# Keys of two early projections in shared PSUM banks, the second input loaded in two halves, and a new order of the first steps

## The chip, the cores and the metric

The kernel runs on one core of a Trainium2 chip. A core has five engines that work side by side, each through its own list of instructions in order: TensorE (PE, matrix products into PSUM), VectorE (DVE), ScalarE (ACT, exponentials and copies), GpSimd (POOL, here products in SBUF) and SyncE (SP, which here only issues transfers). Transfers between HBM and SBUF run on 16 DMA engines. An engine waits on semaphores for results of the others. The metric is the time of one execution on the device in microseconds (us); lower is better.

## The reference

Attention with random features, and then a soft mixture of experts over its result:

```python
def phi(x):
    proj = np.einsum('bhsd,df->bhsf', x, w_phi)
    proj = proj - np.max(np.abs(proj), axis=-1, keepdims=True)
    return np.concatenate([np.exp(proj), np.exp(-proj)], axis=-1)
q_p, k_p = (phi(q), phi(k))
kv = np.einsum('bhsf,bhsd->bhfd', k_p, v)
z = np.sum(k_p, axis=2)
num = np.einsum('bhsf,bhfd->bhsd', q_p, kv)
den = np.einsum('bhsf,bhf->bhs', q_p, z)[..., None] + 1e-06
x = num / den                                # as (4608, 512)
...
logits = x @ phi                             # 32 slots
slot_input = softmax_over_tokens(logits).T @ x
h = np.maximum(slot_input[e] @ w1[e], 0.0)   # 8 experts, 4 slots each
slot_out[e] = h @ w2[e]
out = softmax_over_slots(logits) @ slot_out
```

q, k and v have 8 batches, 8 heads, 576 tokens and 64 columns; there are 128 random features. The change touches the start of the attention only.

## The kernel before, in words

The host packs k and q, transposed, into 37 inputs `xT[e]` of 128 partitions by 1024 columns (512 KB; the first is loaded in its two used quarters, 128 KB each). Input e feeds the projections 2e (columns 0 to 511) and 2e + 1 (columns 512 to 1023). A projection (`proj`, matmuls on L281) makes the keys of four token tiles, and the queries of the four tiles that lie two projections back: `proj` b writes keys `kx[b]` into a PSUM bank of the pool `psk`, which has two, and from b = 2 on queries `qx[b - 2]` into a bank of `mm` (two as well). The halves of the 128 partitions hold keys and queries and trade places with each projection.

What follows for the keys of one projection b:

- `kneg_exp` b (ACT, L312), `kmax` b (DVE, L286, the largest absolute value per token) and `kpos_exp` b (ACT, L315) read the bank. No two engines read one bank at a time: for the first two projections the order is `kneg_exp`, `kmax`, `kpos_exp`. The two exponentials make the tile `kf`.
- `kfac` b (ACT, L289 and L290) takes exponentials of the maxima, into `mk`.
- `vals` p (POOL, L301) multiplies value tiles `vt[u]` (325 KB of input for one head of two batches, loaded by `vload` u) with `mk`, into `vs`. The pieces 0, 1 and 2 are the four, four and one tiles of the first head; pieces 3 and 4 begin the second.
- `kvmm` p (PE, L328) multiplies `kf` with `vs` and sums into `kvp`; `kvcopy` takes the sum out after piece 2.

Queries go through `qpos` (ACT, L348), `qabs` (DVE, L343) and `qneg` (ACT, L351), again one after the other on their bank, then `num` (PE, L381) multiplies them with the copied sum, and DVE and POOL finish the attention. Later PE turns the tokens, makes logits, runs both expert layers (L850, L925) and the output (L945).

Three more PSUM banks are shared (`bank3`, tokens `nm`: one in the pool `pmo`, two in `pnum`): whoever takes one gets the one that came free longest ago. The results of `num`, the transposes and logits use them. `spin` (L206) is a matmul on a constant (`warm`) whose result nobody reads: nine stand at the very start, in banks of `mm`, and eight more (`NSPIN`) among the first steps, in the shared banks.

The order is written out by hand. Each letter of the string `ORDER` issues the next task of one kind; `LETTERS` says which. Every engine runs its tasks in the order of the string. The planner `Plan` hands out tokens for buffers and banks and checks that the listed predecessors were issued; the costs and due times in the calls of `add` are not used when the order is given. On the chip the waits follow from what the tiles share. Before, the first steps are on PE: `proj` 0, 1, six spins, `proj` 2, a spin, `proj` 3, `kvmm` 0, 1, a spin, `kvmm` 2, `proj` 4, 5; on ACT: `kneg_exp` 0, 1, `kpos_exp` 0, `kfac` 0, 1, `kpos_exp` 1, `qpos` 0, `kneg_exp` 2, `qpos` 1, `qneg` 0, `kfac` 2, `kpos_exp` 2, `kneg_exp` 3, `qneg` 1, `kpos_exp` 3, `kneg_exp` 4; on DVE: `kmax` 0, 1, `qabs` 0, `kmax` 2, 3, `qabs` 1.

The first transfers are issued before the string is run: on SP's queue the quarters of input 0 (L197, L199) and the whole input 1 (`xload(1)`, L174); on ACT's queue the projection matrix `wd` (L198) and value tile 0 (L189). Inputs 2 and 3, value tile 1 and so on follow on SP's queue.

Of the kernel before, what the change touches and what calls it, by code (L numbers as in the profile page):

```python
# [9 lines left out]
F32 = mybir.dt.float32  # L10
# [6 lines left out]
B, H, S, D = 8, 8, 576, 64  # L17
# [5 lines left out]
NCH = NT // CH  # L23
# [5 lines left out]
XW = 8 * 128  # L29
# [9 lines left out]

NB = NU * NT // 4  # L40
NWARM = 9
NSPIN = 8
NFIN = 3
TRI = 3
BUFS = {'xs': 3, 'kf': 3, 'vs': 2, 'vt': 2, 'qf': 3, 'un': 2, 'xT': 4, 'xc': 2}
# [11 lines left out]
class Plan:  # L57
# [10 lines left out]
    def add(self, kind, key, engine, cost, fn, after=(), get=(), put=(), lat=0.0, at=0, mode=None):  # L68
        get, put = ([(g, None) if isinstance(g, str) else g for g in x] for x in (get, put))
        self.tasks.setdefault(kind, []).append((key, fn, after, get, put))  # L70
# [29 lines left out]
ORDER = (  # L100
    "bcceafeefedhdggehjibecikbajelfcmdbmdknghjefomilcbunhfipoghclrjqddlrmkjagmjsnbkifnthijgvovmwcljofpwqdgcrvrmkjwnlm"
    "yhksomfdpnathixrvwvczolijwgfcrlhaqkdAvAgrmjnAbkwfbyomstizhcArfvwnlkjnAdorimdavAgcowhjpiqvcgwdfbmhgjyrlrdslxjztvf"
    "AknmivhiknawgowmcofjplcAhrjrAmdvqwxdlgjiykfrnakmgmostcvnbhpvjiwwlfocdjzqsArlvhkntrgbmdwAAvwomkfigcdryjharvznfkmi"
    "bowcvlpwjrghAqrmdnlijAAykofsmnhiczotxjvwgkdlvcfmgAwjqfjparrhsdmnmvgAtwAojlxihmkvyzwnorvjwpbrvwcfAixckmybdfazAnrh"
    "AdgliABABgjljCoqxcBCskhtBCmilmnfCdrDEkonvchpFwgvlwqoibcrrjdjkafbAnmhodsvkmwBitgCBcBvwCxlBylCfrnhfjrivmvhCwjDGdzx"
    "oEcwaqkipsndoFcgglHGjHIJrIymfKhKkAgldnqgbtLisojmArAvwfhkvimtpnjcojwzcrfalhvdgrmdwlkfAAnmAbjmJvwhoprkvMwyirjgjzcv"
    "wnlyAoifcdamdkqAnmlhixgzfoxsAtjrhjLviwrcgvlbmknoArfawvAjpqwxhycmklfbmnshrkdzidAtnorvcwAlivggjocmfajwrqMAprjdvhwk"
    "mknsdiynmgrAtzjfAogclvAwhoAljfiqdvgcwmrhkjpdvsftwxlnryvmgimazwrhkbjvowrnaiAvAmjpwocckymfnzdbAAhrdglBNjlCBgoiqCkf"
    "cBbsBAjmthAifmlnCrCdkhnvjiwxvwoDcoaEcBpbFbdgflBjxhrdCrNmvqxmskfnwCiBlCBhtgCojicaGxvfklDrnwdohxOrEkgnjFqvwiymvpcw"
    "gocHjHdzmIfgyrzJGkIsdlKLhnKmAfArjhlAmtvwiovAkiwAcnAjobacpqdgfglsrrvhmfjbknltwvOwmdyrvkjjgnraxvwimwzphocikocdfyrl"  # L110
    "ghirAdjqnlkszPxAAmfonojtmjvhwigmcvwdMjpcNArrflagkdmqhnsimfgljAkhAmvtwjopcfvyrJwjbirlanqdzkmAmAvvhnocsoAMiwtwbgcf"
    "yzbAjralNlfvhwAkrdiAmdkpnbxnvoghroqvjgwjcwdfsligycxtrdkzhvrminmvoAfjlmawgjcrfLApwlbjhvkqwryhmkAminzonAsBBcodticA"
    "gCCvdfjwBCfBrlrhlCAdkvniokhmjvnqxiwbDgwcoOEcFBBprlglsajytdmCmvjmxqknCfwPzHpgBIBjChmCrsjdgjfoPJvrkiDwhvEwKncFiMbd"
    "fGAohcHLylrtlgkaIqmAmJndsgKoijcfAzvwrdNkpvfwnrbvmAwahjhlirogAAtriknvjwvcwGyfOljzxkdonoxcmmghlqpriAvwbkrbjdysxAmA"
    "tznrcfhvgkndvwiwjofcaAlAlmmrhgpqdAkvfrjmwsnMohriitayLckvocvnwgrkdwnvjwxmjzffAglmplocyhjhAzNocxxAAqRldSRlmjrsmgkS"
    "APjOtPvmqprwvRrwSnvwiOTURsAQRkSotyrSnRvoVQwRVzrSSrvwyyTAARUzPASvzARXASwyXRYzA4XZYSY0X2QYZ0TZ73W905Q5682236573Q5+"
    "695W5888++8/W+<=/Q!=!i!!")

# [7 lines left out]
def tile_kernel(ctx: ExitStack, tc, xT, vv, w, phi, w1, w2, cst, out):  # L126
# [46 lines left out]
    def load(t, x):  # L173
        i = nc.sync.dma_start(t, x).ins  # L174
        if len(sent) > 5 and len(wpools) < 2:
            tc.add_manual_dep(i, sent[-2].name, mybir.DependencyInfo(mybir.DependencyClass.Sync, mybir.DependencyReason.DATA), reason="deep")
        sent.append(i)
# [3 lines left out]
    def xload(e):  # L181
        if e > 2:
            xs[e] = xtile(e)
        if e:
            load(xs[e], xT[e])

    def vload(u):
        vt[u] = vp.tile([128, VW], F32, tag="vt", name="vt", bufs=BUFS["vt"])
        load(vt[u], vv[u // H, u % H]) if u else nc.scalar.dma_start(vt[u], vv[u // H, u % H])  # L189


    call = const.tile([128, NTT, NS], F32, name="call")
# [3 lines left out]
    wd = qp.tile([128, FE], F32, name="wd", bufs=1)  # L196
    nc.sync.dma_start(xs[0][0:64, 0:512], xT[0][0:64, 0:512])  # L197
    nc.scalar.dma_start(wd, w)  # L198
    nc.sync.dma_start(xs[0][64:128, 512:XW], xT[0][64:128, 512:XW])  # L199
    vload(0)  # L200
    xload(1)
    nc.gpsimd.memset(call[:, 0:2], 0.0)
    warm = call[:, 0:2].rearrange("p t s -> p (t s)").bitcast(mybir.dt.bfloat16)

# [61 lines left out]
    def proj(b):  # L266
        half = slice(0, 64), slice(64, 128)
        kh, qh = half[::-1] if b % 2 else half
        if b < NB:
            kx[b] = pkp.tile([128, 4, 128], F32, tag="psk", name="psk")  # L270
        if b > 1:
            qx[b - 2] = pmm.tile([128, 4, 128], F32, tag="mm", name="psq")
        x = xs[b // 2].rearrange("p (t i) -> p t i", i=128)[:, 4 * (b % 2):4 * (b % 2) + 4]
        for i in range(4):
            two = []
            if b < NB:
                two.append((kx[b][:, i], x[kh, i], wd[kh]))
            if b > 1:
                two.append((qx[b - 2][:, i], wd[qh], x[qh, i]))
            for ps, l, r in two[::-1] if b % 2 else two:  # L280
                nc.tensor.matmul(ps, l, r, start=True, stop=True)  # L281
# [351 lines left out]
    def zsi(i):  # L633
        nc.vector.tensor_copy(si[:, 2 * i:2 * i + 2], fin["st", i][:, 0:2])
        if i:
# [3 lines left out]


    plan = Plan(dict({k: BUFS[k] for k in ("kf", "vs", "qf", "un", "xT", "xc", "vt")}, xs=BUFS["xs"] - 2, psk=2, psq=2,
                     kb0=1, kb1=1, qb0=1, qb1=1, pkv=1, kvs=2, psn=2, mo=2, mk=6, mh=1, eq=3, dn=3, lT=3, de=2,
                     cd=3, pl=2, pr=3, nm=3))
    add = plan.add

    for e in range(NB // 2 + 1):
        first = e < 2
        add("load", e, SP, 1.35 if e else 1.43, (lambda: None) if first else lambda e=e: xload(e), lat=2.2, at=8 / 3 * e,
            get=[] if first else ["xs"], after=[("vload", 0)] if e == 1 else [])
    for u in range(NU):  # L650
        add("vload", u, SP, 0.85, lambda u=u: vload(u) if u else None, after=[] if u == 0 else [("load", 1)], lat=2.2, at=NCH * u, get=["vt"])

    for b in range(NB + 2):
        def task(kind, engine, cost, fn, key, bank, **k):
            add(kind, key, engine, cost, lambda: fn(key), at=4 / 3 * bank, **k)
        task("proj", PE, 0.896 if 1 < b < NB else 0.77, proj, b, b, after=[("load", b // 2)], lat=0.34, mode="r", get=["psk"] * (b < NB) + ["psq"] * (b > 1), put=["xs"] * (b % 2))
        bank = [f"kb{b % 2}"]
        if b < NB:
            task("kmax", DVE, 0.6, kmax, b, b, after=[("proj", b)], get=["mk"] + bank, put=bank, lat=0.16)
            task("kfac", ACT, 0.19, kfac, b, b, after=[("kmax", b)], lat=0.21)  # L660
            task("kneg_exp", ACT, 0.478, kneg_exp, b, b, after=[("proj", b)], get=["kf"] + bank, put=bank, lat=0.13)
            task("kpos_exp", ACT, 0.478, kpos_exp, b, b, after=[("kneg_exp", b)], get=bank, put=bank)
            task("kread", None, 0.0, lambda b: None, b, b, after=[("kmax", b), ("kpos_exp", b)], put=["psk"], lat=0.0)
        for p, (b_, u, t0, t1) in enumerate(pieces):
            if b_ == b:
                new, end = t0 == 0 or p == 0 or pieces[p - 1][0] != b, 4 * b + 4 == NT * u + t1
                n = t1 - t0
                mid = t0 <= 4 < t1
                task("vals", POOL, 0.14 * (1 + (mid and t1 > t0 + (t0 == 4))) + 0.22 * (n + mid), vals, p, b,
                     after=[("kfac", b), ("vload", u)] + ([] if pieces[p - 1][0] != b else [("vals", p - 1)]),  # L670
                     get=["vs"] * (p == 0 or pieces[p - 1][0] != b), put=["mk"] * end + ["vt"] * (t1 == NT))
                task("kvmm", PE, 0.233 * n + 0.215 * mid, kvmm, p, b, after=[("kpos_exp", b), ("vals", p)] + ([("kvmm", p - 1)] if p else []),
                     get=["pkv"] * (t0 == 0), put=["kf", "vs"] * end, mode="c", lat=0.25)
        q, bank = b - 2, [f"qb{b % 2}"]
        if q >= 0:
            task("qabs", DVE, 0.63, qabs, q, q, after=[("proj", b)], get=bank, put=bank, lat=0.16)
            task("qpos", ACT, 0.478, qpos, q, q, after=[("proj", b)], get=bank + ["qf"], put=bank, lat=0.13)
            task("qneg", ACT, 0.478, qneg, q, q, after=[("qpos", q)], get=bank, put=bank, lat=0.13)
            task("qread", None, 0.0, lambda b: None, q, q, after=[("qabs", q), ("qneg", q)], put=["psq"], lat=0.0)
# [111 lines left out]
        task("wdiv", POOL, 0.36, wdiv, n, after=[("wsum", n)], put=["cd"])  # L791

    for i in range(NSPIN):
        add("spin", i, PE, 0.22 if i > 1 else 0.43, lambda: spin(bank3("spin", [128, 512], "psw"), warm), after=[("proj", 0)], get=["psn", ("nm", "spin")], put=["psn", ("nm", "spin")], lat=0.0, at=1e6)
    add("consts", 0, SP, 0.75, constants, after=[("proj", 4)], at=15, lat=2.5)
    for i in range(nslot[0]):
        add("weight", i, SP, 1.3, lambda: load_w(1), after=[("consts", 0)], at=1000)
# [216 lines left out]
```

## Time and profile before

| | us |
|---|---|
| median of 3 timed runs | 329.48 |
| lowest and highest of them | 328.75, 329.61 |
| profiled execution, its own time | 328.39 |
| its span, first to last instruction | 326.6 |

All times inside the kernel are from the span's start in that one execution. The page of the profile has the busy time and the idle time of groups of instructions; the trace behind it gives the chain of waits (followed back from the last instruction), the timeline, the transfers with their time from issue to landing, and busy times in chosen stretches. In rows of stretches the numbers stand for start and end, length, busy time with the count of instructions of PE, PE's weight loads, DVE, ACT and POOL, then the granted PE clock, the DMA engines' busy share and GB/s. In a row of the timeline the first number is the start, the second the duration (of several merged instructions: from the first's start to the last's end), and in brackets stands how long the engine was idle before and what released it. The engines overlap neighbouring instructions a little, so that a next one can start before the last one's recorded end.

### The profile page before, as it was taken

How to read it: one execution, taken by the hardware profiler on the slowest of the kernel's cores; microseconds unless marked ns; L12 is line 12 of the kernel's file. 1: busy time of each engine (PE TensorE's matmuls, PEld its weight loads, DVE VectorE, ACT ScalarE, POOL GpSimd, SP SyncE). 2: the span in 40 equal slices, each digit the busy share in tenths (PEclk: the TensorE clock that was granted, in tenths of full speed). 3: DMA queues.
4: the chain of work that ended last, by engine and by line, in shares of the span. 5: the costliest groups of instructions: out<-in, count | busy, mean ns of one | idle time of the engine just before them, and what ended most of it. 6: DMA issues, size and time to landing. Idle time of an engine off the chain costs nothing.

```text
span 326.6 us, 16706 instructions
## 1 busy us (share of the span) xinstructions
PE 315.7 (97%) x7095; PEld 269.4 (82%) x7095; DVE 241.2 (74%) x688; ACT 229.3 (70%) x674; POOL 160.9 (49%) x339
## 2 busy tenths in 40 slices
PE   8999999999999999999999999999999999999990
PEld 4899999999979999999799999988999864376640
DVE  1488978877888889779897897968987867433461
ACT  4898979878976988798779986976879451003350
POOL 1556767764267768634567877265668310200000
PEclk9999999999999999999999999999999999999997
DMA  7665574766736664768555567717577999999897
GB/s 248 198 173 175 171 207 121 235 198 207 215 96 185 199 204 141 235 171 244 169 170 174 174 225 192 223 51 237 188 223 258 320 354 310 412 409 366 323 377 298
DMA packets 23130, 74.12 MB, mean 227 GB/s; under 512 B 2576, under 2 KB 2960, under 8 KB 23056
## 3 DMA queue, kind: packets, MB, share of 16 engines
q1 hardware_dynamic: 22768, 72.65, 67.7%
q8 instruction: 56, 0.92, 1.2%
q10 hardware_dynamic: 288, 0.40, 0.4%
q14 instruction: 18, 0.15, 0.1%
HBM read 63.60 MB, written 9.44 MB: 224 GB/s over the span
## 4 chain that ended last, share of the span: by engine, by line
PE 93%; DVE 1%; ACT 1%; issue 1%; DMA 1%; SPq 0%; DVEq 0%; POOL 0%; ACTq 0%; POOLq 0%
PE kvp L328 24%; PE psn L381 22%; PE psq L281 12%; PE psk L281 11%; PE psx L734 5%; PE yp L925 4%; PE hp L850 4%; PE psl L438 3%; PE pso L945 2%; PE pss L470 2%; PE psw L206 2%; DMA out<-o 1%; PE psd L463 1%; PE pss L585 1%; PE psh L903 1%
## 5 line engine op out<-in xcount | busy, mean ns | idle before, releaser
L301 POOL TENSOR_TENSOR vs<-vt,mk 128x520 f32<-128x520 f32 (+3 forms) x128 | 91.5, 730 | 59.5 <-ACT mk L290 42.5
L328 PE MATMUL kvp<-vs,kf 128*64 128x65 f32 (+1 forms) x2304 | 85.7, 229 | 0.0
L328 PEld LDWEIGHTS kvp<-vs,kf 128*64 128x64 f32 x2304 | 78.6, 138 | 4.7 <-issue 1.9
L381 PE MATMUL psn<-kvs,qf 128*64 128x65 f32 x2304 | 79.2, 223 | 0.3 <-issue 0.2
L381 PEld LDWEIGHTS psn<-kvs,qf 128*64 128x64 f32 x2304 | 72.6, 138 | 4.5 <-issue 1.0
L281 PE MATMUL psq<-xs,wd 64*128 64x128 f32 x576 | 75.5, 280 | 0.0
L281 PE MATMUL psk<-wd,xs 64*128 64x128 f32 x576 | 75.3, 280 | 0.1
L281 PEld LDWEIGHTS psq<-xs,wd 64*128 64x128 f32 x576 | 67.2, 187 | 4.1 <-issue 2.1
L281 PEld LDWEIGHTS psk<-wd,xs 64*128 64x128 f32 x576 | 67.0, 187 | 3.1 <-issue 1.6
L286 DVE TENSOR_REDUCE mk<-psk 128x4 f32<-128x512 f32 x72 | 48.2, 679 | 15.9 <-ACT kf L312 9.1
L312 ACT ACTIVATE kf<-psk 128x512 f32<-128x512 f32 x72 | 42.6, 594 | 22.5 <-PE psk L281 8.0
L343 DVE TRANSPOSE_TENSOR_REDUCE mts<-psq 128x16 f32<-128x512 f32 x72 | 50.2, 706 | 8.2 <-PE psq L281 3.5
L348 ACT ACTIVATE qf<-psq 128x512 f32<-128x512 f32 x72 | 42.4, 592 | 10.7 <-PE psn L381 3.0
L427 POOL TENSOR_TENSOR xc<-un,dn 128x256 f32<-128x256 f32 x62 | 37.9, 614 | 13.3 <-DVE dn L412 7.0
L351 ACT ACTIVATE qf<-psq 128x512 f32<-128x512 f32 x72 | 42.4, 594 | 1.7 <-DVE mts L343 1.7
L315 ACT ACTIVATE kf<-psk 128x512 f32<-128x512 f32 x72 | 42.6, 595 | 0.5 <-DVE mk L286 0.5
L392 DVE TENSOR_TENSOR un<-psn,eq 128x195 f32<-128x195 f32 x96 | 33.0, 350 | 10.3 <-PE psn L381 7.5
L397 DVE TENSOR_TENSOR un<-psn,un 128x195 f32<-128x195 f32 x96 | 33.4, 354 | 1.9
L359 ACT ACTIVATE mh<-mts 32x36 f32<-32x36 f32 x128 | 29.4, 229 | 2.4 <-DVE mts L343 0.6
L365 DVE TENSOR_REDUCE eq<-mh 32x9 f32<-32x36 f32 x128 | 26.1, 204 | 5.2 <-ACT mh L359 3.9
L949 DVE COPY o<-pso 128x384 f32<-128x384 f32 x24 | 12.1, 552 | 13.0 <-PE pso L945 13.0
L949 ACT COPY o<-pso 128x384 f32<-128x384 f32 x24 | 10.2, 484 | 11.7 <-PE pso L945 10.7
(121 smaller groups left out, 317.9 us busy)
## 6 DMA issues: line engine op xcount, KB each, us to landing
wt<-w SPq DMA_DIRECT2D x64, 512.0 KB, 5.6
xs<-xT SPq DMA_DIRECT2D x36, 512.0 KB, 4.4
vt<-vv SPq DMA_DIRECT2D x31, 325.0 KB, 3.2
out<-o SPq DMA_DIRECT2D x24, 384.0 KB, 4.2
vt<-vv ACTq DMA_DIRECT2D x1, 325.0 KB, 3.2
xs<-xT SPq DMA_DIRECT2D x2, 128.0 KB, 3.3
cs<-cst SPq DMA_DIRECT2D x1, 128.0 KB, 4.2
wd<-w ACTq DMA_DIRECT2D x1, 64.0 KB, 1.8
```

The lines of the kernel that those rows point to most:

```text
L281: nc.tensor.matmul(ps, l, r, start=True, stop=True)
L286: nc.vector.tensor_reduce(km[b][:, 2], kx[b], axis=AX, op=ALU.max, apply_absolute_value=True)
L301: nc.gpsimd.tensor_tensor(vs[b][:, :, place(b, u, t, o):place(b, u, t, o) + n], v[:, t + o:t + o + n].unsqueeze(1).broadcast_to([128, 2, n ...
L312: nc.scalar.activation(kf[b][:, 1], kx[b], AF.Exp, scale=-1.0)
L315: nc.scalar.activation(kf[b][:, 0], kx[b], AF.Exp)
L328: nc.tensor.matmul(ps[f:f + FE // 2, pn, o:o + m], kf[b][:, pn, NT * u + t - 4 * b, f:f + FE // 2], v2[:, pn, at:at + m], start=(t == 0 an ...
L343: nc.vector.tensor_reduce(mts.rearrange("p r j -> p j r")[:, o:o + 4], qx[b].rearrange("p j (r t) -> p (j r) t", t=32), axis=AX, op=ALU.ma ...
L348: nc.scalar.activation(qf[b][:, 0], qx[b], AF.Exp)
L351: nc.scalar.activation(qf[b][:, 1], qx[b], AF.Exp, scale=-1.0)
L381: nc.tensor.matmul(ps[64 * f:64 * f + 64, j, pn], q2[:, pn, 64 * f:64 * f + 64], kv[:, pn, b2], start=True, stop=True)
L397: nc.vector.tensor_tensor(x, nx.pop(s)[:, :, 1], x, op=ALU.add)
L427: divider(u).tensor_tensor(x[:, :, h * D:(h + 1) * D], un[u][:, a:b, 0:64], dn[u][:, a:b].unsqueeze(2).broadcast_to([128, b - a, 64]), op= ...
```

## The change

- The keys of the projections 2 and 3 (`EARLY`) no longer go into a `psk` bank but into a shared one, taken with a token `("nm", ("kx", b))` and given back by `kread` b when `kmax` b and `kpos_exp` b have been issued. The names `kb2` and `kb3` stand for their banks in the plan.
- `NSPIN` goes from 8 to 3. The order on PE is now: `proj` 0, 1, three spins, `proj` 2, 3, `kvmm` 0, 1, 2, `proj` 4, 5. Between any two tasks of ACT, DVE or POOL the order is as it was, and from `qread` 0 and `kvmm` 2 on the string is the same letter by letter.
- Input 1 is loaded in two halves by columns (0 to 511, 512 to 1023), each of 256 KB. On SP's queue now come: the first quarter of input 0, the first half of input 1, value tile 0, the second half of input 1, then input 2 and value tile 1 as before. On ACT's queue come `wd` and the second quarter of input 0; value tile 0 has left it.
- Value tile 0 now enters the list `sent` of numbered loads in place of input 1, so that the list stays as long as it was.
- The other edits change costs and predecessors in the plan, which with a written order are only checked.

The diff, without the strings whose letters only moved across lines:

```diff
-NSPIN = 8
+NSPIN = 3
+EARLY = 2, 3
...
-    "bcceafeefeedhdggehjibecikbajelfcmdbmdknghjefomilcb
...
+    "bccefeefdhdgghibajcikbajlfcmdbmdknghjfomilcb
...
     def xload(e):
         if e > 2:
             xs[e] = xtile(e)
-        if e:
+        if e > 1:
             load(xs[e], xT[e])
 
     def vload(u):
         vt[u] = vp.tile([128, VW], F32, tag="vt", name="vt", bufs=BUFS["vt"])
-        load(vt[u], vv[u // H, u % H]) if u else nc.scalar.dma_start(vt[u], vv[u // H, u % H])
+        load(vt[u], vv[u // H, u % H])
...
     nc.sync.dma_start(xs[0][0:64, 0:512], xT[0][0:64, 0:512])
     nc.scalar.dma_start(wd, w)
-    nc.sync.dma_start(xs[0][64:128, 512:XW], xT[0][64:128, 512:XW])
+    nc.scalar.dma_start(xs[0][64:128, 512:XW], xT[0][64:128, 512:XW])
+    xload(1)
+    nc.sync.dma_start(xs[1][:, 0:512], xT[1][:, 0:512])
     vload(0)
-    xload(1)
+    nc.sync.dma_start(xs[1][:, 512:XW], xT[1][:, 512:XW])
...
-            kx[b] = pkp.tile([128, 4, 128], F32, tag="psk", name="psk")
+            kx[b] = bank3(("kx", b), [128, 4, 128], "psk") if b in EARLY else pkp.tile([128, 4, 128], F32, tag="psk", name="psk")
...
-                     kb0=1, kb1=1, qb0=1, qb1=1, pkv=1, kvs=2, psn=2, mo=2, mk=6, mh=1, eq=3, dn=3, lT=3, de=2,
+                     kb0=1, kb1=1, kb2=1, kb3=1, qb0=1, qb1=1, pkv=1, kvs=2, psn=2, mo=2, mk=6, mh=1, eq=3, dn=3, lT=3, de=2,
...
+        place_ = [("nm", ("kx", b))] if b in EARLY else ["psk"]
-        task("proj", PE, 0.896 if 1 < b < NB else 0.77, proj, b, b, after=[("load", b // 2)], lat=0.34, mode="r", get=["psk"] * (b < NB) + ["psq"] * (b > 1), put=["xs"] * (b % 2))
-        bank = [f"kb{b % 2}"]
+        task("proj", PE, 0.896 if 1 < b < NB else 0.77, proj, b, b, after=[("load", b // 2)], lat=0.34, mode="r", get=place_ * (b < NB) + ["psq"] * (b > 1), put=["xs"] * (b % 2))
+        bank = [f"kb{b if b in EARLY else b % 2}"]
...
-            task("kread", None, 0.0, lambda b: None, b, b, after=[("kmax", b), ("kpos_exp", b)], put=["psk"], lat=0.0)
+            task("kread", None, 0.0, lambda b: None, b, b, after=[("kmax", b), ("kpos_exp", b)], put=place_, lat=0.0)
```

More of the change, by code (lines that the diff above doesn't have):

```diff
@@ L100 @@
 ORDER = (
[L101 to L115, printed above, removed]
@@ L116 @@
-    "APjOtPvmqprwvRrwSnvwiOTURsAQRkSotyrSnRvoVQwRVzrSSrvwyyTAARUzPASvzARXASwyXRYzA4XZYSY0X2QYZ0TZ73W905Q5682236573Q5+"
-    "695W5888++8/W+<=/Q!=!i!!")
+    "bccefeefdhdgghibajcikbajlfcmdbmdknghjfomilcbunhfipoghclrjqddlrmkjagmjsnbkifnthijgvovmwcljofpwqdgcrvrmkjwnlmyhkso"
+    "mfdpnathixrvwvczolijwgfcrlhaqkdAvAgrmjnAbkwfbyomstizhcArfvwnlkjnAdorimdavAgcowhjpiqvcgwdfbmhgjyrlrdslxjztvfAknmi"
+    "vhiknawgowmcofjplcAhrjrAmdvqwxdlgjiykfrnakmgmostcvnbhpvjiwwlfocdjzqsArlvhkntrgbmdwAAvwomkfigcdryjharvznfkmibowcv"
@@ new lines @@
+    "lpwjrghAqrmdnlijAAykofsmnhiczotxjvwgkdlvcfmgAwjqfjparrhsdmnmvgAtwAojlxihmkvyzwnorvjwpbrvwcfAixckmybdfazAnrhAdgli"
+    "ABABgjljCoqxcBCskhtBCmilmnfCdrDEkonvchpFwgvlwqoibcrrjdjkafbAnmhodsvkmwBitgCBcBvwCxlBylCfrnhfjrivmvhCwjDGdzxoEcwa"
+    "qkipsndoFcgglHGjHIJrIymfKhKkAgldnqgbtLisojmArAvwfhkvimtpnjcojwzcrfalhvdgrmdwlkfAAnmAbjmJvwhoprkvMwyirjgjzcvwnlyA"
+    "oifcdamdkqAnmlhixgzfoxsAtjrhjLviwrcgvlbmknoArfawvAjpqwxhycmklfbmnshrkdzidAtnorvcwAlivggjocmfajwrqMAprjdvhwkmknsd"
+    "iynmgrAtzjfAogclvAwhoAljfiqdvgcwmrhkjpdvsftwxlnryvmgimazwrhkbjvowrnaiAvAmjpwocckymfnzdbAAhrdglBNjlCBgoiqCkfcBbsB"
@@ new lines @@
+    "AjmthAifmlnCrCdkhnvjiwxvwoDcoaEcBpbFbdgflBjxhrdCrNmvqxmskfnwCiBlCBhtgCojicaGxvfklDrnwdohxOrEkgnjFqvwiymvpcwgocHj"
+    "HdzmIfgyrzJGkIsdlKLhnKmAfArjhlAmtvwiovAkiwAcnAjobacpqdgfglsrrvhmfjbknltwvOwmdyrvkjjgnraxvwimwzphocikocdfyrlghirA"
+    "djqnlkszPxAAmfonojtmjvhwigmcvwdMjpcNArrflagkdmqhnsimfgljAkhAmvtwjopcfvyrJwjbirlanqdzkmAmAvvhnocsoAMiwtwbgcfyzbAj"
+    "ralNlfvhwAkrdiAmdkpnbxnvoghroqvjgwjcwdfsligycxtrdkzhvrminmvoAfjlmawgjcrfLApwlbjhvkqwryhmkAminzonAsBBcodticAgCCvd"
+    "fjwBCfBrlrhlCAdkvniokhmjvnqxiwbDgwcoOEcFBBprlglsajytdmCmvjmxqknCfwPzHpgBIBjChmCrsjdgjfoPJvrkiDwhvEwKncFiMbdfGAoh"
@@ L121 @@
+    "cHLylrtlgkaIqmAmJndsgKoijcfAzvwrdNkpvfwnrbvmAwahjhlirogAAtriknvjwvcwGyfOljzxkdonoxcmmghlqpriAvwbkrbjdysxAmAtznrc"
+    "fhvgkndvwiwjofcaAlAlmmrhgpqdAkvfrjmwsnMohriitayLckvocvnwgrkdwnvjwxmjzffAglmplocyhjhAzNocxxAAqRldSRlmjrsmgkSAPjOt"
+    "PvmqprwvRrwSnvwiOTURsAQRkSotyrSnRvoVQwRVzrSSrvwyyTAARUzPASvzARXASwyXRYzA4XZYSY0X2QYZ0TZ73W905Q5682236573Q5+695W5"
+    "888++8/W+<=/Q!=!i!!")
 COLS = 128
@@ L647, in tile_kernel @@
         first = e < 2
-        add("load", e, SP, 1.35 if e else 1.43, (lambda: None) if first else lambda e=e: xload(e), lat=2.2, at=8 / 3 * e,
-            get=[] if first else ["xs"], after=[("vload", 0)] if e == 1 else [])
+        add("load", e, SP, (2.5, 0.65)[e] if first else 1.35, (lambda: None) if first else lambda e=e: xload(e), lat=2.2, at=8 / 3 * e,
+            get=[] if first else ["xs"], after=[("load", 0)] if e == 1 else [])
     for u in range(NU):
-        add("vload", u, SP, 0.85, lambda u=u: vload(u) if u else None, after=[] if u == 0 else [("load", 1)], lat=2.2, at=NCH * u, get=["vt"])
+        add("vload", u, SP, 0.85, lambda u=u: vload(u) if u else None, after=[("load", 1)], lat=2.2, at=NCH * u, get=["vt"])
     for b in range(NB + 2):
@@ L671, in tile_kernel @@
                      get=["vs"] * (p == 0 or pieces[p - 1][0] != b), put=["mk"] * end + ["vt"] * (t1 == NT))
-                task("kvmm", PE, 0.233 * n + 0.215 * mid, kvmm, p, b, after=[("kpos_exp", b), ("vals", p)] + ([("kvmm", p - 1)] if p else []),
+                task("kvmm", PE, 0.233 * n + 0.215 * mid, kvmm, p, b, after=[("kpos_exp", b), ("vals", p)] + ([("kvmm", p - 1)] if p else []) + ([("spin", NSPIN - 1)] if p == 3 else []),
                      get=["pkv"] * (t0 == 0), put=["kf", "vs"] * end, mode="c", lat=0.25)
@@ L793, in tile_kernel @@
     for i in range(NSPIN):
-        add("spin", i, PE, 0.22 if i > 1 else 0.43, lambda: spin(bank3("spin", [128, 512], "psw"), warm), after=[("proj", 0)], get=["psn", ("nm", "spin")], put=["psn", ("nm", "spin")], lat=0.0, at=1e6)
+        add("spin", i, PE, 0.22, lambda: spin(bank3("spin", [128, 512], "psw"), warm), after=[("proj", 0)], get=["psn", ("nm", "spin")], put=["psn", ("nm", "spin")], lat=0.0, at=1e6)
     add("consts", 0, SP, 0.75, constants, after=[("proj", 4)], at=15, lat=2.5)
```

## The prediction

> **What bounds the kernel now.** I read the page first, for the engine that sets the time.
>
> ```profile
> PE 315.7 (97%) x7095; PEld 269.4 (82%) x7095; DVE 241.2 (74%) x688; ACT 229.3 (70%) x674; POOL 160.9 (49%) x339
> PE 93%; DVE 1%; ACT 1%; issue 1%; DMA 1%; SPq 0%; DVEq 0%; POOL 0%; ACTq 0%; POOLq 0%
> PE pso L945 <- ACT yt L937: 0.7, 1, 0.7
> ```
>
> The first line is busy time, the second the engines' shares of the chain that ended last, the last the longest of PE's own waits behind its first matmul. PE is busy 97% of the span and carries 93% of the chain; nowhere does it wait longer than 0.7 us. So an idle or wasted microsecond on PE is a microsecond of the kernel. But "busy" counts L206 too, the matmuls on a constant whose result nobody reads (`spin`). Where they stand, PE is really waiting. So next the chain of waits over the first 14 us (start, duration, what):
>
> ```profile
> 0.94 3.91 PE psw L206 x9
> 4.85 1.10 PE psk L281 x11
> ...
> 5.98 0.60 ACT kf L312
> ...
> 6.61 0.70 DVE mk L286
> ...
> 7.33 0.61 ACT kf L315
> ...
> 7.98 0.37 PE psk L281
> ...
> 9.14 0.32 PE psw L206
> ...
> 10.56 2.23 PE kvp L328 x64
> 12.78 0.32 PE psw L206
> 13.11 0.38 PE kvp L328 x8
> ```
>
> The chain leaves PE at 5.95 and comes back at 7.98: `kneg_exp` 0 (ACT), `kmax` 0 (DVE) and `kpos_exp` 0 (ACT) read the first keys' bank one after the other, and only then may `proj` 2 write its keys there, since `psk` has two banks. After that PE never leaves the chain, but two spins (9.14, 12.78) lie in it. The timeline shows what fills the hole and when the other engines are ready:
>
> ```profile
> 6.43 1.47 PE L206 MATMUL psw<-call 128*128 128x512 bf16 x6
> 8.19 2.42 POOL L301 TENSOR_TENSOR vs<-vt,mk 128x520 f32<-128x520 f32 x3 [6.75 <-ACT mk L290]
> 8.21 0.58 ACT L315 ACTIVATE kf<-psk 128x512 f32<-128x512 f32 x1
> 9.21 0.60 ACT L348 ACTIVATE qf<-psq 128x512 f32<-128x512 f32 x1 [0.43 <-PE psq L281]
> 9.84 0.72 DVE L343 TRANSPOSE_TENSOR_REDUCE mts<-psq 128x16 f32<-128x512 f32 x1 [1.95 <-ACT qf L348]
> 11.99 1.20 POOL L301 TENSOR_TENSOR vs<-vt,mk 128x130 f32<-128x130 f32 x2 [1.37 <-ACT mk L290]
> 12.70 0.62 ACT L351 ACTIVATE qf<-psq 128x512 f32<-128x512 f32 x1
> 13.18 0.63 ACT L315 ACTIVATE kf<-psk 128x512 f32<-128x512 f32 x1
> 14.67 0.60 ACT L312 ACTIVATE kf<-psk 128x512 f32<-128x512 f32 x1 [0.86 <-PE psq L281]
> ```
>
> **The change, part by part.** I place each PE step anew, up to the start of `proj` 4, which was at 13.11 + 0.38 = 13.49.
>
> *Spins and banks.* Of eight spins three are left, all behind `proj` 1: six took 1.47, so 0.245 each, and three end at 6.43 + 0.74 = 7.17. `proj` 2 writes keys into a shared `nm` bank that only a PE spin has used, so neither ACT nor DVE holds it; its queries' bank was last a warm spin's. It took 7.98 to 9.14 = 1.16, so now 7.17 to 8.33. The spin behind it is gone; `proj` 3 took from 9.46 to 10.56 = 1.10, so now 8.33 to 9.43.
>
> *What is late next.* `kvmm` 0 needs `vals` 0, first of the three POOL instructions at 8.19. These wait for `kfac` 0 on ACT, behind `kpos_exp` 0 in an ACT order that is the same: they don't move. Three instructions end at 8.19 + 2.42 = 10.61. By widths (520, 130, 520) the first has some 1.05 of it and ends at 9.25, ahead of 9.43. Of the 2.23 of the first 64 value matmuls I give 1.03 to `kvmm` 0 (32 narrow ones) and 1.20 to `kvmm` 1 (eight of its 32 are double width). `kvmm` 0 is done at 10.46; `kvmm` 1 must wait for POOL until 10.61, and I add 0.06 for the release: 10.67 to 11.87. So POOL takes back 0.2 of the gain. The stall could be nothing (10.46) or, if POOL's rough span hides 0.3 more, 0.5; I take the row.
>
> *`kvmm` 2* needs `vals` 2, which hangs on `kfac` 2, behind `kmax` 2, `qpos` 1 and `qneg` 0. ACT first: back to back the exponentials start 0.48 apart (12.70, 13.18), so `kpos_exp` 1 at 8.21 lets `qpos` 0 start at 8.69 (`proj` 2 is done at 8.33), before at 9.21. `qabs` 0 follows at 9.32, `kmax` 2 one DVE step later (0.72 in the row, 0.64 without the overlap) at 9.96, done by 10.63; ACT has gone through `kneg_exp` 2, `qpos` 1 and `qneg` 0 by 10.65; so `kfac` 2 at 10.7, `vals` 2 from some 11.05 to 11.45. That is 0.4 ahead of 11.87, so it hides. The last spin (0.32) is gone. `kvmm` 2 took 0.38 behind it: 12.25 at most. Eight matmuls at the pace of the other narrow ones, 1.03 / 32, would take 0.26: 12.13. I take 12.24 for `proj` 4.
>
> *Queries' banks and ACT afterwards.* `proj` 4 and 5 need `qneg` 0 and `qneg` 1 done, by the same steps 10.8 and 12.5, against 12.24 and 13.3. In the trace ACT idled 0.86 before 14.67 waiting for `proj` 4, and still idles there by about 0.4. From there the order on every engine is the same, and so are the banks: three spins and two key tiles take five turns of the three `nm` banks where eight spins took eight, and both leave the same bank next. From this cut on everything should run as before, 13.49 - 12.24 = 1.25 us earlier.
>
> *The loads.* Now the transfers, by queue time and time to landing, and what moved per microsecond (second last number the DMA share, last GB/s):
>
> ```profile
> 1.97 0.58 SPq L174 DMA_DIRECT2D xs<-xT  x1
> xs<-xT SPq DMA_DIRECT2D x1, 512.0 KB, 5.1
> 3.07 0.43 SPq L174 DMA_DIRECT2D vt<-vv  x1
> vt<-vv SPq DMA_DIRECT2D x1, 325.0 KB, 6.2
> 1.00:2.00 1.00, 1.00 (x3) 0.37 (x4) 0.00 (x0) 0.38 (x1) 0.44 (x3) 1.00 0.13 40
> 2.00:3.00 1.00, 1.00 (x3) 0.30 (x2) 0.00 (x0) 0.90 (x1) 0.00 (x0) 1.00 0.98 240
> 3.00:4.00 1.00, 1.00 (x4) 0.40 (x3) 0.00 (x0) 0.00 (x0) 0.00 (x0) 1.00 1.03 291
> 4.00:5.00 1.00, 1.00 (x5) 0.27 (x3) 0.00 (x0) 0.00 (x0) 0.00 (x0) 1.00 1.04 270
> 5.00:6.00 1.00, 1.00 (x14) 1.00 (x13) 0.00 (x0) 0.02 (x1) 0.00 (x0) 1.00 1.10 373
> ```
>
> From 2 us on the DMA engines are full, so bytes set the landing. Second input before: 64 + 128 + 128 + 325 + 512 KB by the tiles' shapes, 1185 thousand bytes with all ahead of it, had moved by about 5.9; it landed at 1.97 + 5.1 = 7.07, some 1.15 behind its last byte. By the same sum the first half has 590 thousand bytes through its end (4.1, landing 5.2), `vt` 0 923 (5.2, landing 6.4), the second half 1185 (landing 7.1). They are needed at 7.17, 8.19 and 8.33: all hidden, the first by 2 us, the others by 1.2 or more. The bound from the other side is `vt` 1, which went last and landed at 3.07 + 6.2 = 9.3; as late as that, `vt` 0 would delay POOL by 1.1. The half on ACT's queue costs ACT nothing that counts: it only stands ahead of a table load some 4 us early. The extra issue on SP, 0.58, pushes back the third input and `vt` 1, which is hidden behind full DMA engines: `vt` 1 is first wanted by the second POOL instruction of the 11.99 row, now about 11.45.
>
> *Sum.* the 1.55 from 6.43 to 7.98 and twice 0.32, 2.19 in all, become 0.74 of spins and 0.2 of stall: -1.25 (no stall and the short `kvmm` 2: -1.57). The profiled execution, span 326.6, took 328.39 in all; 1.25 less gives 325.35 and 327.14. Its time lies 1.1 below the median of the three timed runs, 329.48, so on that scale the forecast is 328.2. About 0.3% (0.99 us) is what a measurement of this kernel can tell from no change, so the forecast stands not far beyond that line.
>
> **A rule that speaks against it.** Here the row comes first: nine opening spins took 3.91, 0.434 each, six later ones 0.245 each. PE begins slow and is up to pace at about 4.8, though its granted clock is printed as 1.00 from the start. How long it stays so without work shows at the end of the run (fields as above; the clock is third from the end):
>
> ```profile
> 316.00:320.00 4.00, 2.39 (x24) 0.89 (x16) 2.88 (x6) 2.50 (x6) 0.00 (x0) 1.00 1.02 398
> 320.00:324.00 4.00, 0.00 (x0) 0.00 (x0) 0.00 (x0) 0.00 (x0) 0.00 (x0) 0.76 1.01 401
> 324.00:327.00 3.00, 0.00 (x0) 0.00 (x0) 0.00 (x0) 0.00 (x0) 0.00 (x0) 0.50 0.18 69
> ```
>
> The last matmul ends by 318.4; a mean of 0.76 over the next stretch, with 0.50 after it, puts the fall of the clock at about 322.1, some 3.7 us later. The Trainium skill, "TensorE: Matmul & The Clock Gate", Part 1, says that the clock is halved by default, is released by about 3.4 us of sustained work and is throttled again after an idle window of that length; this trace agrees, with 3.9 and 3.7.
>
> **Rivals.**
>
> *Only the spins are saved, not the wait.* If the change doesn't do what it says and `proj` 2 still starts at 7.98 (its bank turns out held), or if `vals` 2 doesn't come earlier than its 11.99, PE loses only the later spins. First case: `proj` 2 and 3 end at 10.24, `kvmm` 0 and 1 at 12.47, just behind `vals` 2 (130 of the 520 columns in the 11.99 row, some 0.4 of its 1.20), and `proj` 4 starts at about 12.85, 0.64 earlier. Second: `kvmm` 2 from 12.45, `proj` 4 at some 12.8, 0.7 earlier. Either: 328.8. For it speaks how full ACT is from 8.2 to 13; against it the 0.4 in hand and the shared banks' history. 0.20.
>
> *`vt` 0 becomes the bound.* Landing as late as `vt` 1 it delays the POOL steps by 1.1 and leaves 0.15: 329.3. The full queue speaks for it, the byte sum against. 0.07.
>
> *The tail takes it back.* DMA is also full late, while weights and outputs pass. If that stretch didn't start earlier with PE, nothing would be left: 329.5. But its slots come free by PE's steps. 0.07.
>
> *The clock falls, and the kernel gets slower.* Place: behind the three spins. If PE fell back for a stretch as long as the opening one, 3.91 us of slow pace would do 3.91 x 0.245 / 0.434 = 2.21 us of work and cost 1.70: with the 1.25 gained, 0.45 slower, 329.9. It decides from an idle stretch of about 3.7 us; I expect 0.2. 0.03.
>
> **How the numbers follow.** The forecast has 0.63. It lies 0.26 beyond the 0.3% line and the three runs spread over 0.86, so I count 0.55 of it as faster, the rest as same; the first rival adds 0.03 to faster: 0.58. The clock rival and plain scatter give slower 0.06; 0.36 is left for same. Range: the full 1.57 with 0.4 of scatter gives 327.5; `vt` 0 as late as `vt` 1 gives 329.3. The tail and the clock stay outside.
>
> **What would show it.** Right: three short spins behind `proj` 1; `proj` 2 at about 7.2 with no release by ACT; POOL still at 8.19; a PE gap of about 0.2 ahead of `kvmm` 1, released by POOL; no spin later; `proj` 4 at 12.2; the span near 325.35. Wrong: `proj` 2 at 7.98 or released by a DMA; POOL waiting for `vt`; a gap ahead of `kvmm` 2; a step 1.25 earlier at 14 us but not at 270; spins or projections at the slow pace after 5 us.

## The result, and the profile after

| | before | changed |
|---|---|---|
| median, first comparison (20 runs each) | 329.43 us | 327.46 us |
| ratio, 95% interval | | 0.9943 (0.9927 to 0.9960) |
| median, second comparison (35 and 12 runs) | 329.13 us | 328.11 us |
| ratio, 95% interval | | 0.9952 (0.9933 to 0.9971) |
| profiled execution, its own time | 328.39 us | 327.53 us |
| its span | 326.6 us | 325.7 us |

The changed kernel is faster: by 1.9 us in the first comparison (2.4 to 1.3 by the interval), by 1.6 in the second (2.2 to 1.0; there the medians alone differ by 1.0). 1.25 was forecast. The profiled execution of banks_spins below ran at a lower granted clock (0.85 in place of 0.99) and is left out, from its median too.

The page after has the same two lines as before, almost unchanged: a change of 1.2 us can't be read from shares.

```profile
PE 314.4 (97%) x7090; PEld 269.1 (83%) x7090; DVE 241.2 (74%) x688; ACT 229.3 (70%) x674; POOL 161.2 (49%) x339
PE 94%; DVE 1%; ACT 1%; POOL 1%; issue 1%; DVEq 0%; ACTq 0%; POOLq 0%
```

The chain of waits over the first 12 us of the changed kernel (start, duration, what) shows what took the place of the old detour:

```profile
0.94 3.50 PE psw L209 x9
4.43 1.10 PE psk L284 x11
...
5.56 0.61 ACT kf L315
...
6.19 0.70 DVE mk L289
...
6.91 0.60 ACT kf L318
...
7.78 2.44 POOL vs L304 x3
...
10.25 1.60 PE kvp L331 x40
11.85 0.30 PE psk L284
```

Before, the chain came back to PE at 7.98, through `proj` 2. Now it goes on from ACT to POOL (`kfac` 0, then `vals` 0 and 1) and comes back at 10.25 through `kvmm` 1: POOL's products are the new bound of the first steps. The timeline of the same stretch:

```profile
6.01 0.82 PE L209 MATMUL psw<-call 128*128 128x512 bf16 x3
6.76 0.37 PE L284 MATMUL psk<-wd,xs 64*128 64x128 f32 x1
7.78 2.43 POOL L304 TENSOR_TENSOR vs<-vt,mk 128x520 f32<-128x520 f32 x3 [6.33 <-ACT mk L293]
8.89 1.15 PE L331 MATMUL kvp<-vs,kf 128*64 128x65 f32 x32
10.25 1.60 PE L331 MATMUL kvp<-vs,kf 128*64 128x130 f32 x40 [0.21 <-POOL vs L304]
10.65 1.21 POOL L304 TENSOR_TENSOR vs<-vt,mk 128x130 f32<-128x130 f32 x2 [0.45 <-ACT mk L293]
13.03 0.60 ACT L315 ACTIVATE kf<-psk 128x512 f32<-128x512 f32 x1 [0.51 <-PE psq L284]
```

`proj` 2 starts right behind the third spin with no release by ACT; PE waits 0.21 for POOL ahead of `kvmm` 1. Everything in this execution stands 0.42 earlier than before already at `kneg_exp` 0 (5.56 against 5.98), ahead of anything that the change touches: the nine warm spins took 3.50 here and 3.91 there. So the steps are compared from `kneg_exp` 0 (ACT's first exponential) to the first matmul of `proj` 4: 5.56 to 11.78 = 6.22 now, 5.98 to 13.42 = 7.44 before (timeline starts). **That is 1.22 us less.** Of the 0.9 us between the two spans, 0.42 is this start and 1.22 the steps; the way from `proj` 4 to the end took 0.8 longer in this execution (314.0 against 313.2; in the other profiles at full clock and without a long stop it lay between 313.2 and 314.6).

The loads of the changed kernel on SP's queue, from the timeline (start, time to issue):

```profile
1.36 0.56 SPq L202 DMA_DIRECT2D xs<-xT  x1
1.98 0.46 SPq L175 DMA_DIRECT2D vt<-vv  x1
2.48 0.43 SPq L204 DMA_DIRECT2D xs<-xT  x1
```

The same three in the view of the transfers, with KB and the time from issue to landing:

```profile
xs<-xT SPq DMA_DIRECT2D x1, 256.0 KB, 3.5
vt<-vv SPq DMA_DIRECT2D x1, 325.0 KB, 3.7
xs<-xT SPq DMA_DIRECT2D x1, 256.0 KB, 5.2
```

The first half of input 1 lands at 4.9, value tile 0 at 5.7, the second half at 7.7; they are wanted at 6.76, 7.78 and 7.76.

### The profile page after: what moved, and what is told of

It reads as the page before. It is cut to its first block, busy times and chain, and to the rows that moved or that the text cites. A ratio compares the mean times of both kernels' runs of the same rounds, so it can differ in the third digit from the quotient of the medians.

```text
span 325.7 us, 16698 instructions
## 1 busy us (share of the span) xinstructions
PE 314.4 (97%) x7090; PEld 269.1 (83%) x7090; DVE 241.2 (74%) x688; ACT 229.3 (70%) x674; POOL 161.2 (49%) x339
## 4 chain that ended last, share of the span: by engine, by line
PE 94%; DVE 1%; ACT 1%; POOL 1%; issue 1%; DVEq 0%; ACTq 0%; POOLq 0%
PE kvp L331 24%; PE psn L384 22%; PE psq L284 11%; PE psk L284 11%; PE yp L929 5%; PE psx L738 5%; PE hp L854 4%; PE pso L949 3%; PE psl L441 3%; PE pss L473 2%; PE psw L209 1%; PE psd L466 1%; POOL vs L304 1%; PE pss L588 1%; PE psh L907 1%
```

## Experiments

Two questions were open: which part of the change does it, and where the gain beyond 1.22 comes from. All times are medians of timed runs against runs of the kernel before on the same chip; "steps" is the time from `kneg_exp` 0 to `proj` 4 in the profiled execution. Three dots in an edit stand for lines not shown. changed_again is the changed kernel in its second comparison; its profile repeats the steps (6.23).

| kernel | median | before | ratio (95%) | steps |
|---|---|---|---|---|
| banks_spins | 328.02 | 329.52 | 0.9954 (0.9934 to 0.9975) | |
| loads_alone | 329.41 | 329.52 | 0.9998 (0.9977 to 1.0019) | 7.44 |
| spins_alone | 328.36 | 329.52 | 0.9975 (0.9956 to 0.9995) | 6.50 |
| no_spins | 329.16 | 329.52 | 0.9979 (0.9947 to 1.0010) | 6.23 |
| changed_again | 328.11 | 329.13 | 0.9952 (0.9933 to 0.9971) | 6.23 |
| no_spins_again | 329.12 | 329.13 | 1.0010 (0.9989 to 1.0031) | 6.22 |
| eight_spins | 328.75 | 329.13 | 0.9990 (0.9973 to 1.0006) | 6.75 |
| kfac_first | 327.67 | 329.13 | 0.9957 (0.9937 to 0.9976) | 5.96 |
| no_spins_pad | 328.26 | 329.65 | 0.9960 (0.9944 to 0.9976) | 6.29 |
| tail_unpadded | 328.47 | 329.65 | 0.9966 (0.9948 to 0.9985) | 6.23 |
| kfac_warm6 | 327.54 | 329.65 | 0.9941 (0.9918 to 0.9964) | 6.48 |
| before_again | 329.04 (one) | | | 8.00 |

### The parts one by one

**banks_spins**: the changed kernel with the old loads.

```diff
...
-    nc.scalar.dma_start(xs[0][64:128, 512:XW], xT[0][64:128, 512:XW])
-    xload(1)
-    nc.sync.dma_start(xs[1][:, 0:512], xT[1][:, 0:512])
-    vload(0)
-    nc.sync.dma_start(xs[1][:, 512:XW], xT[1][:, 512:XW])
+    nc.sync.dma_start(xs[0][64:128, 512:XW], xT[0][64:128, 512:XW])
+    vload(0)
+    xload(1)
```

> The changed kernel with the loads as they were (input 1 whole on SP's queue, value tile 0 on ACT's). Theory of the steps: input 1 lands at about 7.1, so projection 2 is held up by at most 0.4 us, and the 0.2 us in which kvmm 1 waits for POOL anyway takes most of that; within 0.3 us of the changed kernel, 1.0 to 1.25 faster than before by the steps. Rival (the loads bring the part of the 1.97 that the steps don't explain): it loses about 0.7 of the gain and stands at 1.2 faster where the changed kernel stands at 1.9.

1.5 us faster than before; from the changed kernel (0.9943 and 0.9952) it can't be told apart. The loads aren't what the gain rests on, though a few tenths for them are within these intervals.

**loads_alone**: the reverse edit, the new loads in the kernel before.

> The kernel before with the loads of the changed one (input 1 in halves, the first ahead of value tile 0, all three on SP's queue); banks, spins and order as before. Theory of the steps: projection 2 still starts at about 8.0, released by ACT; no difference, 0 +- 0.3 us. Rival (the loads bring the unexplained part): 0.6 to 0.7 us faster.

No difference (0.9998, at most 0.8 us either way), and the steps are those of before to the hundredth, 7.44. As the theory had it.

**spins_alone**: the new order and three spins, keys of `proj` 2 and 3 in `psk` banks, old loads.

```diff
-EARLY = 2, 3
+EARLY = ()
...
```

> The order and the three spins of the changed kernel, with the keys of projections 2 and 3 in psk banks and the loads as before. Theory of the steps: projection 2 waits idle until kpos_exp 0 is done, 7.98 on the clock of the run before; only the two later spins are saved; projection 4 at about 12.85, 0.64 us faster than before. Rival (PE is often still at its slow pace when the six spins behind projection 1 run, so that they take up to 2.6 us in place of 1.5 and hold projection 2 back themselves): 1.2 us or more faster.

0.8 us faster by the ratio. In its timeline PE now stands still where the spins were:

```profile
6.94 0.82 PE L207 MATMUL psw<-call 128*128 128x512 bf16 x3
8.49 0.37 PE L282 MATMUL psk<-wd,xs 64*128 64x128 f32 x1 [0.73 <-ACT kf L316]
10.48 2.59 PE L329 MATMUL kvp<-vs,kf 128*64 128x65 f32 x72
```

The wait for `kpos_exp` 0 is all there, and yet the steps take 6.50 in place of 7.44. `proj` 4 follows `proj` 2 after 4.50 us (8.49 to 12.99), before after 5.44 (7.98 to 13.42): each of the two later spins cost 0.47, not the 0.32 that the chain of waits printed for it. So most of the 1.22 is the two spins, 0.94; the shared banks, with the new loads that spins_alone lacks, add 0.28, because behind them POOL stops the way. This split is that of the steps; in time the intervals of spins_alone and of the changed kernel overlap.

**eight_spins**: the changed kernel with eight spins behind `proj` 1.

```diff
-NSPIN = 3
+NSPIN = 8
...
-    "bccefeefdhdgghibajc
+    "bccefeeeeeeefdhdgghibajc
```

> The changed kernel with eight spins behind projection 1 in place of three. Theory of the steps: five more spins of 0.245 take 1.2 us, of which the 0.2 us in which kvmm 1 waits for POOL goes under; from kneg_exp 0 to projection 4 it takes 6.2 + 1.0 = 7.2 us, and the kernel is 1.0 us slower than the changed one, 0.2 to 0.3 faster than before. Rival (POOL bounds the steps and hides them): no slower than the changed kernel.

The steps grew by 0.53, not by 1.0 (6.75): the eight spins held `proj` 2 back, and PE caught up behind them, since its way from `proj` 2 to `proj` 4, with no spin in it, is 4.47 (8.50 to 12.97) where the changed kernel, waiting for POOL, needs 5.02 (6.76 to 11.78). So spins at this place cost less than their length. By the steps 0.69 of the 1.22 is left; the ratio, 0.9990 (0.9973 to 1.0006), allows 0.9 us of gain and none.

```profile
6.67 1.90 PE L209 MATMUL psw<-call 128*128 128x512 bf16 x8
```

### No spins at all: the steps right, the time wrong

**no_spins** and **no_spins_again** are one kernel: the changed one without its three early spins.

```diff
-NSPIN = 3
+NSPIN = 0
...
-    "bccefeefdhdgghibajc
+    "bccffdhdgghibajc
...
```

> The changed kernel without its three spins behind projection 1. Theory of the steps: projections 2 and 3 and kvmm 0 come 0.7 to 0.8 us earlier, but kvmm 1 waits for the same POOL instruction, with a PE gap of about 0.9 us in place of 0.2; projection 4 starts when it does in the changed kernel, time the same within 0.3 us. Rival (PE, not POOL, sets the pace in most executions): 0.5 us or more faster than the changed kernel.

> The changed kernel without the three spins once more: in the first comparison its steps were those of the changed kernel (6.23 us from kneg_exp 0 to projection 4), yet its median was higher by more than 1 us and its times were spread widely. Theory of the steps: within 0.5 us of the changed kernel this time. Rival (the spins keep PE's clock up: without them PE idles for 1 us at 9 to 10 us, and in some executions the clock falls or opens later): again 1 us or more above the changed kernel, with some executions 3 us or more above its fastest.

The steps take 6.23 as with the spins, as the theory said. `proj` 2 comes early, but `kvmm` 0 doesn't, against the theory: PE waits 1.05 for POOL ahead of it, and 0.22 ahead of `kvmm` 1. The granted clock stays at 1.00 through this wait (8 to 13 us), so the rival of no_spins_again has the time right, 1.0 us above the changed kernel, and the cause wrong.

```profile
9.02 2.43 POOL L304 TENSOR_TENSOR vs<-vt,mk 128x520 f32<-128x520 f32 x3 [7.57 <-ACT mk L293]
10.13 1.15 PE L331 MATMUL kvp<-vs,kf 128*64 128x65 f32 x32 [1.05 <-POOL vs L304]
```

But the medians, 329.16 and 329.12, are close to those of the kernel before (329.52 and 329.13), and both intervals hold 1. The loss isn't in the first steps. The chain of waits near 294 us, first of no_spins, then of the changed kernel:

```profile
293.95 0.42 PE psy L940 x2
294.37 0.45 PE yp L929 x9
294.81 1.83 issue
296.64 0.65 PE yp L929 x7
297.29 1.59 PE pso L949 x8
```

```profile
293.00 0.42 PE psy L940 x2
293.42 0.35 PE yp L929 x7
...
294.04 0.52 PE yp L929 x9
```

In the second expert layer PE stops for 1.83 us in the middle of 16 equal matmuls, with "issue" as releaser: no semaphore ended it. Second profile: 1.57. All other profiles at full clock up to then have a stop at this spot too, of 0.16 to 0.39. It lies at the same count of PE instructions in every kernel (13505 or 13506 of them from the start), not at the same matmul. The queue of instruction transfers (q8) shows a 16 KB transfer a little ahead of it: it starts at 291.59 in the changed kernel, 1.35 before the two `psy` matmuls, but at 294.03 in no_spins, when they had begun (293.88), and PE goes on 2.45 and 2.61 us after the transfer's start (294.04, 296.64). The DMA engines are full there (share 1.02 or more). The link holds beyond this spot: in the 13 profiles at full clock PE has 23 stops of 0.10 us or more that no semaphore ended, and each of them ends 2.2 to 2.6 us behind the start of a transfer on q8.

The Trainium skill, "Runtime: NRT & Kernel Launch", "Instruction fetch mechanics", says that each engine's program is refilled in 16 KiB blocks of 256 instructions, fetched while the current one runs, and that crossing a block is mostly hidden. The blocks are seen here (16,384 bytes each, 56 in a run); that they are hidden holds for most (one to three stops of 0.10 us or more in a profile), not for this one.

So a second theory: three spins fewer are six PE instructions fewer, and by that the fetch of this block begins only with `psy`. Two kernels tell it apart from any harm done by the missing spins themselves.

**no_spins_pad**: no early spins, but six in place of three of the spins that stand shortly before the expert layers, so that the count of instructions is as in the changed kernel.

```diff
-NSPIN = 3
-NFIN = 3
+NSPIN = 0
+NFIN = 6
...
```

> The changed kernel without its three early spins, but with six in place of three of the spins shortly before the expert layers, so that PE's program is as long again ahead of the second expert layer. In both profiles without early spins PE stood 1.6 to 1.8 us in the second expert layer (L929), behind a fetch of 16 KB of instructions that began only after the two matmuls psy ahead of it, where it began 1.2 to 1.4 us before them in all others. Theory (where a page of instructions ends decides when its fetch begins): the wait is 0.2 to 0.4 us again, and the time is within 0.5 us of the changed kernel plus up to 0.6 for the three added spins. Rival (fewer early spins harm the clock or something else in the first steps): the long wait stays, or the time stays at that of the kernel before without it.

**tail_unpadded**: early spins as in the changed kernel, the later three taken out.

```diff
-NFIN = 3
+NFIN = 0
...
```

> The changed kernel with its early spins, but without the three spins shortly before the expert layers: PE's program is six instructions shorter ahead of the second expert layer, as in the kernel without early spins. Theory (page of instructions): the long wait of 1.5 us or more appears in L929 although the first steps are as in the changed kernel (6.2 us from kneg_exp 0 to projection 4), and the time is 0.5 to 1.5 us above the changed kernel. Rival (the early spins decide): the wait stays at 0.2 to 0.4 us, and the time falls by up to 0.6.

The stop follows the count, not the spins: 0.54 in no_spins_pad, 1.48 in tail_unpadded, whose chain is

```profile
293.22 0.42 PE psy L940 x2
293.64 0.55 PE yp L929 x10
294.19 1.48 issue
295.67 0.42 PE yp L929 x6
```

The times go with it: no_spins_pad is 1.3 us below before where no_spins had nothing, though its ratio (0.9960) and that of tail_unpadded (0.9966) are too near to each other and to the changed kernel's to rank them: tail_unpadded has also saved three spins, recorded with 0.38 each. In no_spins_pad PE waited 1.33 for the second half of input 1 ahead of `proj` 3, nearly all of it hidden by POOL (steps 6.29). Shown is the stop and what moves it. Why its fetch begins only with `psy` is not shown. Those two matmuls need a copy by DVE; in the three profiles with the long stop the fetch began 1.0 to 1.1 us behind the end of this copy (293.00 to 294.03 in no_spins), in all others ahead of its end. A request that stands behind the wait for the copy would fit that, but PE itself ran without a stop up to `psy`, 0.9 us behind the copy, so no wait is seen on the engine.

### Trying to move the new bound

**kfac_first**: POOL starts earlier if `kfac` b doesn't stand behind `kpos_exp` b on ACT.

```diff
-    "bccefeefdhdgghibajc
+    "bccefeefdghdghibajc
```

> The changed kernel with kfac 0 and kfac 1 each issued ahead of kpos_exp 0 and kpos_exp 1 on ACT, so that POOL can start about 0.5 us earlier; all else as in the changed kernel. Theory of the steps (after the change POOL's vals 0 and 1 set when kvmm 1 starts): POOL's first product starts 1.7 us behind kneg_exp 0 in place of 2.2, the gap of PE ahead of kvmm 1 goes, and projection 4 starts 0.2 to 0.4 us earlier, 5.8 to 6.0 us behind kneg_exp 0. Rival (PE or kfac 2 on ACT sets it): 6.2 as before, with the wait moved to kvmm 2.

```profile
8.30 2.43 POOL L304 TENSOR_TENSOR vs<-vt,mk 128x520 f32<-128x520 f32 x3 [6.86 <-ACT mk L293]
9.91 2.69 PE L331 MATMUL kvp<-vs,kf 128*64 128x65 f32 x72
11.65 1.21 POOL L304 TENSOR_TENSOR vs<-vt,mk 128x130 f32<-128x130 f32 x2 [0.93 <-ACT mk L293]
```

POOL starts 1.73 behind `kneg_exp` 0 (6.57) in place of 2.22; the 72 value matmuls run without a stop that the timeline prints; the steps fall to 5.96, by 0.26. `kvmm` 2 began at 12.15, just behind `vals` 2 (done at 12.06), so the rival's wait is near. In time that is too little to see: 0.9957.

**kfac_warm6**: besides, six warm spins in place of nine, with the three put before the expert layers (`NFIN` 6) to keep the count.

```diff
-NWARM = 9
-NFIN = 3
+NWARM = 6
+NFIN = 6
...
```

> The order with kfac ahead of kpos_exp, and six in place of nine warm spins at the very start, with six spins before the expert layers so that PE's program stays as long. Theory: input and matrix have landed at 3.4, so projection 0 starts at about 3.6 in place of 4.9, still at PE's slow pace; kneg_exp 0 starts 0.5 to 1.2 us earlier than in the kernel with kfac first, and the time is 0.3 to 1 us below it. Rival (the pace of PE is released later when fewer full matmuls run at the start): projections 0 and 1 take all of it back, no gain.

`kneg_exp` 0 starts at 5.00, the earliest of all, and the span, 324.6, is the shortest. The second half of input 1 now is what comes last. In the chain of waits:

```profile
2.47 5.41 DMA xs<-xT
```

In the view of PE's waits (total, times, longest):

```profile
PE psq L284 <- DMA xs<-xT: 0.6, 1, 0.6
```

Its steps of 6.48 hold this wait of 0.56. The median, 327.54, is 2.1 below before (0.9941); against the changed kernel's 0.9943 and 0.9952 no gain is proved. It isn't shown to beat it.

**before_again**: the kernel before, a second profile.

> The kernel before once more, for a second profile of it. Theory: 7.4 us from kneg_exp 0 to projection 4, as in the first; the start of kneg_exp 0 (5.98 there) anywhere between 5.5 and 7.0, since PE's slow pace at the start ends at another time in each execution.

The steps were not 7.4 but 8.00, and the release that says why was not in the first profile. The timeline, and the view of the transfers:

```profile
8.64 0.34 PE L281 MATMUL psk<-wd,xs 64*128 64x128 f32 x1 [0.65 <-DMA xs<-xT]
```

```profile
xs<-xT SPq DMA_DIRECT2D x1, 512.0 KB, 6.5
```

Input 1, issued at 1.98, landed at 8.5 in place of 7.07, and `proj` 2 waited for it. In the four profiles with the old loads it landed at 6.5, 7.1, 8.0 and 8.5; its first half, in the ten with the new loads, between 4.8 and 4.9 each time. The second half scattered as widely as the whole had: it landed between 6.5 and 8.8.

## Why the prediction was right, point by point

- **The wait for the first keys' bank goes.** Right. Less the 0.42 by which the execution started earlier, the forecast's times are 6.75 for `proj` 2, 10.25 for `kvmm` 1 and 11.82 for `proj` 4 (read from the chain of waits); measured 6.76, 10.25 and, in the chain, 11.85. `proj` 3 and `kvmm` 0 came 0.15 and 0.12 earlier than forecast, in the shadow of POOL: `vals` 0 was done at 8.83, as forecast, and `kvmm` 0 began at 8.89.
- **POOL is late next and takes 0.2 back.** Right: 0.21, released by POOL. no_spins shows it from the other side: `proj` 2 came 1.1 us earlier, and that bought nothing in the steps.
- **`vals` 2 hides.** Right: done by 11.06 in the changed kernel, `kvmm` 2 began at 11.45. In kfac_first, with POOL earlier, it is close to the bound (12.06 against 12.15).
- **A later spin costs 0.32.** Too small: 0.47 (spins_alone). It did not spoil the sum, because POOL sets the start of `kvmm` 1 whatever the spin ahead of it had cost, and the way from there to `proj` 4 was forecast as 1.57 and took 1.60. It does turn round which part matters. The forecast gave the spins alone 0.64 and left 0.61 for the banks; of the 1.22 us measured, 0.94 are two spins and 0.28 the banks. That these two errors cancel follows from POOL's time, not from a right price of each part.
- **The loads cost and bring nothing.** Right for the kernel that I had in view (loads_alone: 0.9998), but the landing of input 1 at 7.07 was one draw of 6.5 to 8.5. In an execution like before_again the old loads cost another 0.56 of steps, which the first half ahead of the value tile should save (no run measures that alone). I had not counted that: a term valued at nothing that is sometimes half a us. The byte sum missed too: the second half was to land at 7.1, 1.2 ahead of its use, and landed at 7.7, just ahead of `proj` 3 (7.76); in no_spins_pad and kfac_warm6 PE waited 1.33 and 0.56 for it.
- **From the cut on all runs 1.25 earlier.** Not shown by this pair of executions: 1.64 earlier at `proj` 4 (1.22 and the 0.42 of the start), 1.24 at the first expert layer (271.94 against 273.18), 1.1 at the last matmul, 0.9 at the end. That 1.24 meets the forecast is luck, since less the 0.42 of the start only 0.82 is left there. On the way PE lost 0.15 and 0.10 in stops like that of the second expert layer; where the rest went is open. The way from `proj` 4 to the end differs by 1.4 us between profiles, so what carries through has to be read from the timed runs.
- **The rivals.** The wait stayed in none of the changed kernel's profiles; value tile 0 landed at 5.7, far from 9.3; the tail took part of it back in this pair (0.8), but not in the timed runs. The clock rival didn't come: PE idled 0.2. Its threshold of 3.7 us of idleness was one reading of many (see the end).
- **The size.** 1.25 forecast and 1.22 measured in the steps, against 1.9 (1.3 to 2.4) and 1.6 (1.0 to 2.2) in time. The second interval holds 1.22, the first just doesn't; 327.46 lies at the lower edge of the range, 328.11 near the 328.2. Late landings of input 1 before are a candidate for the rest, seen in one of two profiles of before; how often they come was not measured, and loads_alone, which loads the first half early, gained nothing in time. Parts of a few tenths can't be told apart by these runs. This stays open.

## What to carry to other kernels

Compare two profiles from an event that the change can't move, not by their spans: here the same nine matmuls at the start shifted everything by up to 1.4 us from one execution to the next, more than the change was worth. A filler matmul that looks free can be on the path where its engine is the bound, and its price is what the neighbours lose, to be had by taking it out. When a kernel with right steps has a wrong time, look for stops with no releaser far from the edit: instructions added or taken away move the borders at which the program is fetched.

## What the hardware showed that I had not expected

- **Fetching PE's program can stop it.** A stop of 0.16 to 0.54 in the second expert layer in ten profiles, of 1.48, 1.57 and 1.83 in the three whose program is six instructions shorter ahead of it than the changed kernel's; the fetch started 2.3 to 2.6 us before PE went on, among full DMA engines.
- **PE's slow pace at the start ends at another time in each execution.** `kneg_exp` 0, behind the same work, began between 5.56 and 6.98 in the profiles with nine warm spins. The trace's record of the granted clock begins, with 1.00, at 3.76 in the first of these and at 6.79 in the last (4.62 in the first profile of before); ahead of its first entry the views print 1.00 as well.
- **The clock can fall after a shorter idle time than the end of the run suggests.** In the first profile of before the fall came about 3.7 us behind the last matmul, but over the 13 profiles at full clock between 1.6 (spins_alone) and 4.6 (tail_unpadded). In no_spins the trace's record has half the clock from 296.55 to 299.96: it fell 1.74 us into the stop of 1.83 (the clock is third from the end):

```profile
292.00:296.00 4.00, 2.81 (x83) 2.33 (x76) 0.29 (x1) 0.27 (x1) 0.00 (x0) 1.00 1.02 401
296.00:300.00 4.00, 3.36 (x39) 1.81 (x42) 1.02 (x2) 0.86 (x2) 0.00 (x0) 0.57 0.40 156
```

  In no_spins_again, after 1.57, it stayed at 1.00; the way from `proj` 4 to the end took 315.0 there and 316.6 in no_spins. The Trainium skill, "TensorE: Matmul & The Clock Gate", Part 1, gives an idle window of about 3.4 us that runs freely. The lengths of the record's entries, whole multiples of 3.41 us (3.41, 23.89, 314.03, 317.44), fit such windows, but a fall 1.6 or 1.74 us after the last matmul doesn't fit a full window of idleness. How much of a window must be idle is not settled here.
